# Expert 5's weights issued earlier, gathers issued in a row, and every expert's second layer on TensorE column tiles of 32

## The chip, the core and the metric

The kernel runs on one core of one Trainium2 chip. The core has TensorE (PE, with its weight loads, PEld), VectorE (DVE), ScalarE (ACT), GpSimd (POOL) and SyncE (SP), which only issues transfers here, and 16 DMA engines that move data between HBM and SBUF. The metric is the device time of one execution in microseconds (us), less is better.

## The reference

Attention with normalised queries and keys, and behind it a layer of experts of which each token uses one, and each expert at most 80 tokens:

```python
q_n, k_n = rmsnorm(q, g_q), rmsnorm(k, g_k)          # (8, 12, 448, 64)
attn = softmax(q_n @ k_n.T / sqrt(64))
x = (attn @ v).transpose(0, 2, 1, 3).reshape(3584, 768)
logits = x @ w_gate                                  # 8 experts
expert_idx, gate_w = argmax(logits), softmax(logits) at expert_idx
out = zeros
for e in range(8):
    tok = the 80 tokens of expert e with the largest gate_w
    h = relu(x[tok] @ w1[e])                         # 768 -> 1024
    out[tok] = gate_w[tok] * (h @ w2[e])             # 1024 -> 768
```

## The kernel before

**Attention.** The 8 batches of 12 heads are 24 groups of four heads, worked through in slots of a schedule that is written out by hand. A group's scores (L436), exponentials (L439), sums (L471) and attention products (L453) run over seven blocks of keys. The rows of x go to a scratch tensor in HBM, `xr_scratch`, with the softmax sums' inverses `rz` beside them. The gate and the choice of the 80 tokens per expert are carried from batch to batch (`merge`), and the last batch's choice stands between the attention and the experts (L934 to L1179).

**Weights.** All expert weights are cast to bf16. Experts 0 to 2 are loaded into place during the attention. Experts 3 to 7 are staged in HBM (`wb_scratch`) and fetched by SP: 3 and most of 4 into space that the queries and keys leave (`weights_early`), the rest of 4 and all of 5 into the space that the attention's own tiles leave (`weights_late`, called in the last slot), 6 and 7 into the space of experts 0 and 1, once those are done. An expert's first layer is `w1` (6 x 128 rows of 1024), its second `w2` (8 x 128 rows of 768), 1536 KB each. SP issues in program order, and one issue that waits holds up all behind it. The stack `av_stack` holds, in this order, `vp0` (values, two buffers), `qkT0`, `vp1` (one buffer of values, used by every third group, the last one too), `qkT1`, `attn` (six buffers of exponentials) and `sm`. Into the same space `weights_late` puts the rest of expert 4, then expert 5's `w1` and `w2`; a tile waits for the last reader of what it lies over.

**The last part of expert 5's `w2`.** `fetch_part` fetches six of the eight blocks after the attention's schedule, and the other two when a DVE memset has released them, which stands behind the first multiply of `normal(1)` (L941, L1260).

**Experts.** For expert e, 48 matmuls make the first layer (`ph`, L1249, 80 columns each), ACT applies the relu, and `xpose(e + 1)` turns the next expert's rows (six transposes). `gather(e)` fetches 80 rows of x from `xr_scratch` with an indirect transfer on POOL's queue, and `normal(e)` scales them on DVE. Gathers 2 and 3 are issued after half of expert 0's first layer, 4 to 7 by experts 0 to 3 as their buffers come free. The second layer (L1224) is, for experts 1 to 7, `main`, the first 64 tokens on two column tiles of 64 (16 matmuls of 384 columns), and `rest`, the other 16 tokens on four column tiles of 32, once for two experts (32 matmuls of 384 columns; expert 7's alone has 32 of 192). Expert 0's second layer takes all 80 tokens at once, 16 matmuls of 384 columns, with `xpose(1)` inside it. DVE multiplies by the gate weight (`yo`, `yr`), and POOL scatters the rows into the output (L1217). For the two column tiles the gate weights and row numbers are spread over the partitions by 12 matmuls (`psp`, L1160).

Of the kernel before, what the change touches and what calls it, by code (L numbers as in the profile page):

```python
# [10 lines left out]
F32 = mybir.dt.float32  # L11
BF16 = mybir.dt.bfloat16
AF = mybir.ActivationFunctionType
ALU = mybir.AluOpType
# [7 lines left out]
def kernel(  # L22
# [185 lines left out]
    NE = DC - 1  # L208

# [11 lines left out]
    def chunk(e, i, c):  # L221
        ts = w_tiles[e][i]
        return ts[0][:, c] if len(ts) == 1 or c < NE else ts[1][:, c - NE]

# [48 lines left out]
    vpools, qktpools = [], []  # L273
    for last in range(2):
        vpools.append(av_stack.enter_context(tc.tile_pool(name=f"vp{last}", bufs=2 - last)))
        qktpools.append(av_stack.enter_context(tc.tile_pool(name=f"qkT{last}", bufs=1)))
    apool = av_stack.enter_context(tc.tile_pool(name="attn", bufs=6))
    smpool = av_stack.enter_context(tc.tile_pool(name="sm", bufs=4))
    with av_stack:
# [506 lines left out]
        def weights_late():  # L786
# [3 lines left out]
            load_weights(wlate, NW0 + 2, NW0 + 2)  # L790
            fetch_late(NW0 + 1)
            fetch_late(NW0 + 2, (0, ))
            mlate.append(ctx.enter_context(tc.tile_pool(name="moe_sb", bufs=2)))
# [142 lines left out]
    FE = FC - 2  # L936

    def fetch_part(c, held=False):
        t = w_tiles[NW0 + 2][1][0]
        if held:  # L940
            nc.vector.memset(t[:, c.start, 0:2], 0.0)  # L941
        nc.sync.dma_start(out=t[:, c], in_=staged(NW0 + 2, 1)[:, c])

    fetch_part(slice(0, FE))
# [4 lines left out]
    xbn = [mpool.tile([128, NT, 256], BF16, tag="yo", name="xbn", bufs=3) for _ in range(NQ)]  # L949
# [169 lines left out]
    outs = dram_disjoint_views(out, E + E // 2)  # L1119
# [20 lines left out]
    idxT = tpool.tile([CAP, 1], U32, name="idxT")  # L1140
    nc.vector.tensor_copy(idxT[:, :], psc[:CAP, 1, :1])
# [5 lines left out]
    gwT = rows[:, 0]  # L1147
# [6 lines left out]
    spread = mpool.tile([128, 2 * E + E], F32, tag="spread", name="spread", bufs=1)  # L1154
    psp = [hot[-1][:, 1, :2 * E], hot[-1][:, 1, 2 * E:3 * E]]
    for o, c in enumerate((slice(0, MT), slice(LT, CAP))):
        n = c.stop - c.start
        for p in range(0, 128, n):
            es = slice(1 + p // 64, None, 2) if o else slice(0, E)
            nc.tensor.matmul(psp[o][p:p + n].rearrange("p (c e) -> p c e", c=2), ident[:CAP, c],  # L1160
                             rows[:, :, es], start=(o == 0), stop=(o == 1))
# [9 lines left out]
    nc.vector.tensor_copy(spread[:, :], hot[-1][:, 1, :3 * E])  # L1171
# [4 lines left out]
    idxP = mpool.tile([128, E // 2], U32, tag="idxP", name="idxP", bufs=1)  # L1176
    for c, x, k in ((slice(0, E // 2 - 1), 2.0, 1), (slice(E // 2 - 1, E // 2), 4.0, 2)):
        nc.vector.tensor_scalar(idxP[:, c], spread[:, 2 * E + E // 2:][:, c], x, off[:, k:k + 1],
# [48 lines left out]
    def main(e, py, fcs):  # L1227
        for fc in fcs:
            for n in range(2):
                product(py[MT * n:MT * n + MT, :], e, fc, slice(0, MT),  # L1230
# [113 lines left out]
```

## Time and profile before

| | us |
|---|---|
| median of three runs | 409.56 (407.32 to 410.78) |
| the profiled execution | 410.17 |
| its span, first to last instruction | 408.5 |
| PE busy | 394.2 (96%) |
| DVE busy | 350.1 (86%) |
| ACT busy | 321.0 (79%) |
| POOL busy | 90.7 (22%) |

Times in the rows below are us from the start of the span. "L1249" is a line of the kernel. In a timeline a row merges like instructions that follow each other on one engine; a bracket at its end is the idle time before it and what ended that. PE is busy nearly throughout, so the shares of the whole span tell little; what matters is who waits in the last 60 us. The ends of matmuls are modelled, and a few records are missing.

### The profile page before, as it was taken

The page shows a single profiled execution, that of the slowest core. Times are in us where ns is not written, and L with a number is a line of the kernel's source. Part 1 is how long each engine was busy: PE and PEld are TensorE (multiplying, and loading weights), DVE is VectorE, ACT ScalarE, POOL GpSimd, SP SyncE. Part 2 cuts the span into 40 slices and gives each one's busy share as a digit, 9 for nine tenths or more (in the row PEclk, how much of TensorE's full clock was granted, in tenths as well). Part 3 has the DMA queues.
Part 4 walks back from the last instruction along what each step waited for, and adds up shares of the span by engine and source line. Part 5 has one row for each costly group of instructions (what it writes and reads, how often), then busy time and mean ns, then how long its engine had stood idle before and what let it go on. Part 6 is the DMA issues. An engine that isn't in the chain of part 4 may idle for free.

```text
span 408.5 us, 12889 instructions
## 1 busy us (share of the span) xinstructions
PE 394.2 (96%) x5407; PEld 191.7 (47%) x5407; DVE 350.1 (86%) x654; ACT 321.0 (79%) x510; POOL 90.7 (22%) x161
## 2 busy tenths in 40 slices
PE   8999999999999999999999999999999999999992
PEld 7434444444444444444444444444444453467771
DVE  4899987998999999997999999979999958875641
ACT  5898979997989889988899699979897877572120
POOL 7300002501031012220251024010510020145522
PEclk9999999999999999999999999999999999999999
DMA  7359999999989999989999999999999269788991
GB/s 245 132 168 198 279 291 253 285 212 308 254 221 265 248 256 273 294 183 238 253 302 214 256 252 229 302 233 290 231 275 292 71 216 373 255 235 239 341 359 66
DMA packets 76266, 100.94 MB, mean 247 GB/s; under 512 B 8536, under 2 KB 65376, under 8 KB 76208
## 3 DMA queue, kind: packets, MB, share of 16 engines
q1 hardware_dynamic: 60192, 70.99, 54.5%
q0 software_dynamic: 16016, 29.13, 38.8%
q8 instruction: 42, 0.69, 0.6%
q14 instruction: 16, 0.13, 0.1%
HBM read 101.11 MB, written 40.23 MB: 346 GB/s over the span
## 4 chain that ended last, share of the span: by engine, by line
PE 69%; DVE 12%; ACT 7%; issue 6%; POOL 3%; DMA 1%; POOLq 0%; DVEq 0%
PE ps L436 26%; PE po L453 25%; PE zl L488 5%; DVE sm L471 4%; PE tp L394 4%; PE xp L394 3%; POOL out_dram L1217 2%; DVE ms L327 2%; DVE qn L357 2%; PE wps L908 2%; DMA xg<-xr_scratch,idxG 1%; ACT at L439 1%; ACT qkT L425 1%; PE mp L679 1%; PE mp L394 1%
## 5 line engine op out<-in xcount | busy, mean ns | idle before, releaser
L439 ACT ACTIVATE at<-ps 128x896 f32<-128x896 f32 x168 | 146.6, 931 | 4.5 <-PE ps L436 3.3
L436 PE MATMUL ps<-qkT 64*64 64x448 f32 x1344 | 147.3, 548 | 2.5 <-ACT row L637 1.3
L453 PE MATMUL po<-at,vt 64*64 64x448 f32 x1344 | 142.5, 537 | 0.0
L471 DVE TENSOR_TENSOR sm<-sm,at 128x896 f32<-128x896 f32 x120 | 130.6, 1088 | 3.1
L453 PEld LDWEIGHTS po<-at,vt 64*64 64x64 f32 x1344 | 50.1, 133 | 74.0 <-issue 63.9
L436 PEld LDWEIGHTS ps<-qkT 64*64 64x64 f32 x1344 | 43.8, 132 | 66.6 <-issue 26.2
L327 DVE TENSOR_REDUCE ms<-sq 128x14 f32<-128x896 f32 (+1 forms) x50 | 52.0, 1041 | 6.8 <-ACT sq L320 6.7
L357 DVE TENSOR_TENSOR qn<-qk,rs 128x896 f32<-128x896 f32 (+1 forms) x47 | 50.6, 1078 | 1.3
L320 ACT ACTIVATE sq<-qk 128x896 f32<-128x896 f32 (+1 forms) x48 | 44.7, 931 | 1.9 <-DMA qk<-in_q_dram 1.1
L240 POOL COPY mark<-mark 1x1 bf16<-1x1 bf16 x18 | 7.1, 393 | 132.0 <-DVE mark L239 132.0
L756 ACT COPY xb<-xp 128x1024 f32<-128x1024 f32 x24 | 24.3, 1012 | 8.5 <-PE xp L394 8.4
L394 PEld LDWEIGHTS tp<-ident,qn 64*128 64x128 f32 x672 | 23.5, 139 | 12.1 <-issue 5.3
L394 PE MATMUL tp<-ident,qn 64*128 64x64 f32 x672 | 27.2, 226 | 0.3 <-DVE qn L357 0.3
L460 ACT COPY us<-po 128x896 f32<-128x896 f32 (+1 forms) x24 | 21.4, 893 | 6.5 <-PE po L453 6.5
L469 DVE TENSOR_TENSOR sm<-at 128x896 f32<-128x896 f32 x24 | 26.0, 1083 | 0.1
L1256 ACT ACTIVATE h_sb<-ph 128x320 bf16<-128x320 f32 x16 | 7.0, 437 | 24.2 <-PE ph L1249 22.3
L425 ACT COPY qkT<-tp 128x896 f32<-128x896 f32 x24 | 22.0, 916 | 3.8 <-PE tp L394 3.7
L423 ACT ACTIVATE qkT<-tp,gqk 128x896 f32<-128x896 f32 x23 | 23.5, 1023 | 0.0
L1224 PE MATMUL py<-w_sb,h_sb 128*64 128x384 bf16 (+3 forms) x256 | 18.6, 318 | 2.2 <-DMA w_sb<-wb_scratch 2.2
L488 PE MATMUL zl<-us,wgs 64*32 64x448 f32 x192 | 20.3, 541 | 0.0
L488 PE MATMUL zl<-sm,zsel 64*32 64x448 f32 x192 | 20.1, 540 | 0.0
L394 PEld LDWEIGHTS xp<-ident,us 64*128 64x128 f32 x384 | 14.0, 139 | 12.0 <-ACT at L439 10.6
(214 smaller groups left out, 425.4 us busy)
## 6 DMA issues: line engine op xcount, KB each, us to landing
vt<-in_v_dram SPq DMA_DIRECT2D x24, 448.0 KB, 6.4
out_dram<-zeros SPq DMA_DIRECT2D x28, 384.0 KB, 8.4
w_sb<-wb_scratch SPq DMA_DIRECT2D x7, 1536.0 KB, 14.7
qk<-in_q_dram SPq DMA_DIRECT2D x23, 448.0 KB, 7.0
qk<-in_k_dram SPq DMA_DIRECT2D x23, 448.0 KB, 6.0
w_sb<-in_moe_w_dram POOLq DMA_DIRECT2D x6, 1536.0 KB, 15.7
xr_scratch<-xb SPq DMA_DIRECT2D x48, 192.0 KB, 6.5
wb_scratch<-in_moe_w_dram POOLq DMA_DIRECT2D x12, 768.0 KB, 9.8
```

The lines of the kernel that those rows point to most:

```text
L320: nc.scalar.activation(o, x, AF.Square)
L327: nc.vector.reduce_sum(out=st[g]["ms"][:, a, lo:hi], in_=st[g]["sq%d" % a][:, lo:hi], axis=AX.X)
L357: e.tensor_mul(qn[:].rearrange("p (x hh) d -> p hh x d", hh=2)[:, h0:h1], qk[:, lo:hi].rearrange("p (hh x) d -> p hh x d", x=NX), rs[:, lo ...
L394: nc.tensor.transpose(o, w, one[p, p], tile_position=(p.start, 0))
L425: nc.scalar.copy(T[:], tp[:, :, :S])
L436: nc.tensor.matmul(ps[u * 64:u * 64 + 64, hh, :S], T1[d, u, x * 64:(x + 1) * 64], T0[d, u, :], start=True, stop=True)
L439: nc.scalar.activation(at[:], ps[:, :, :S], AF.Exp)
L453: nc.tensor.matmul(po[u][hh * D:(hh + 1) * D, u, :S], vt[p, hh * NX + x, :], at[p, hh, :], start=(x == 0), stop=(x == RD - 1))
L469: nc.vector.tensor_add(s["sm"][:], s["at0"][:], s["at1"][:])
L471: nc.vector.tensor_add(s["sm"][:], s["sm"][:], s["at%d" % x][:])
L488: nc.tensor.matmul(t[32 * c:32 * c + 32, r, :S], w, x, start=(i == 0), stop=(i == NQ - 1))
L756: nc.scalar.copy(xb[:].rearrange("p j (u hh d) -> p hh (j u) d", u=2, hh=2), xp[:].rearrange("p hh (k d) -> p hh k d", d=D))
```

## The change

It does five things.

1. `vp1` is the last pool of `av_stack` instead of the third, so that expert 5's `w1` lies over `qkT1` and two buffers of `attn`. Expert 5's `w2` is two tiles, of six and of two blocks. The six are fetched in `weights_late`, right behind `w1` and so ahead of the last two groups' stores in SP's queue; the two where the six were fetched before, with no hold.
2. Gathers 3, 4, 5 and 7 are issued right behind gather 2; gather 6 follows in expert 1.
3. `main` runs on four column tiles of 32 (32 matmuls of 384 columns) for every expert.
4. Expert 0 does as the others: `main(0)`, then `xpose(1)`, `yo` and its scatter, then `rest` of expert 0 alone (32 matmuls of 192 columns), `yr` and its scatter, then `normal(2)`. The copy `idxT` is gone, four small matmuls spread expert 0's last 16 tokens, and there is one more index column.
5. The ring of `yo` has four buffers instead of three, and the output one more disjoint view.

```diff
-    for last in range(2):
-        vpools.append(av_stack.enter_context(tc.tile_pool(name=f"vp{last}", bufs=2 - last)))
+    vpools.append(av_stack.enter_context(tc.tile_pool(name="vp0", bufs=2)))
+    for last in range(2):
         qktpools.append(av_stack.enter_context(tc.tile_pool(name=f"qkT{last}", bufs=1)))
     apool = av_stack.enter_context(tc.tile_pool(name="attn", bufs=6))
     smpool = av_stack.enter_context(tc.tile_pool(name="sm", bufs=4))
+    vpools.append(av_stack.enter_context(tc.tile_pool(name="vp1", bufs=1)))
...
             load_weights(wlate, NW0 + 1, NW0 + 1, gst[0]["w"])
-            load_weights(wlate, NW0 + 2, NW0 + 2)
+            w_tiles[NW0 + 2] = ([wlate.tile([128, DC, F], BF16, tag="w1_5", name="w1_sb")],
+                                [wlate.tile([128, n, DM], BF16, tag=f"w2_5{n}", name="w2_sb")
+                                 for n in (FE, FC - FE)])
             fetch_late(NW0 + 1)
             fetch_late(NW0 + 2, (0, ))
+            nc.sync.dma_start(out=w_tiles[NW0 + 2][1][0][:], in_=staged(NW0 + 2, 1)[:, :FE])
...
-    fetch_part(slice(0, FE))
+    nc.sync.dma_start(out=w_tiles[NW0 + 2][1][1][:], in_=staged(NW0 + 2, 1)[:, FE:])
...
-    idxT = tpool.tile([CAP, 1], U32, name="idxT")
-    nc.vector.tensor_copy(idxT[:, :], psc[:CAP, 1, :1])
...
+    for p in range(0, 128, 32):
+        nc.tensor.matmul(hot[-1][p:p + 32, 1, 3 * E:3 * E + 2], ident[:CAP, LT:CAP],
+                         rows[:, :, 0], start=False, stop=True)
...
     def main(e, py, fcs):
         for fc in fcs:
-            for n in range(2):
-                product(py[MT * n:MT * n + MT, :], e, fc, slice(0, MT),
-                        slice(n * DN, n * DN + DN))
+            for n in range(4):
+                t, c = n % 2 * 32, n // 2 * DN
+                product(py[32 * n:32 * n + 32, :], e, fc, slice(t, t + 32), slice(c, c + DN))
...
                 gather(2, ph[:CAP, 0, 0:1])
-                gather(3)
+                for n in (3, 4, 5, 7):
+                    gather(n)
...
-                xn = normal(1, lambda: fetch_part(slice(FE, FC), True))
+                xn = normal(1)
         if 0 < e < E - 1:
             xpose(e + 1, xn)
-        if e < E - 4:
-            gather(e + 4, wait=True)
+        if e == 1:
+            gather(6, wait=True)
...
+        py = sums("py")
+        main(e, py, fcs)
         if e == 0:
...
+            xpose(1, xn)
+        yo = mpool.tile([128, DN], F32, tag="yo", name="yo", bufs=4)
+        nc.vector.tensor_scalar(yo[:, :], py[:, :], gws[:, e:e + 1], None, op0=ALU.mult)
+        scatter(e, idxM[:, e:e + 1], yo[:, :], 2)
+        if e % 2 == 0 or e == E - 1:
+            k = (e - 1) // 2 if e else E // 2
+            g = gwP[:, k:k + 1] if e else spread[:, 3 * E:3 * E + 1]
+            single = e in (0, E - 1)
+            pair = (e, ) if single else (e - 1, e)
             w = len(pair) * DM // 4
             pz = sums("pz")
             rest(pair, pz, fcs)
...
+        if e == 0:
+            xn = normal(2)
```

## Rows read from the trace of the kernel before

**Rows 1.** Timeline of PE, 364 to 403 us: start, us, engine, line, operation, tiles, count
```profile
364.79 0.47 PE L1160 MATMUL hot<-rows,ident 80*64 80x16 f32 x12
365.19 1.89 PE L1249 MATMUL ph<-xgT,w_sb 128*128 128x80 bf16 x48
366.94 2.14 PE L1224 MATMUL py<-w_sb,h_sb 128*80 128x384 bf16 x12
369.32 0.92 PE L1203 MATMUL pxt<-identb,xn 80*128 80x80 bf16 x6 [0.24 <-DVE w_sb L941]
...
370.74 1.88 PE L1249 MATMUL ph<-xgT,w_sb 128*128 128x80 bf16 x48
...
374.19 1.89 PE L1249 MATMUL ph<-xgT,w_sb 128*128 128x80 bf16 x48
...
376.23 2.90 PE L1224 MATMUL py<-w_sb,h_sb 128*64 128x384 bf16 x48
379.07 1.89 PE L1249 MATMUL ph<-xgT,w_sb 128*128 128x80 bf16 x48
...
389.38 0.50 PE L1249 MATMUL ph<-xgT,w_sb 128*128 128x80 bf16 x9 [0.40 <-issue]
...
400.15 1.17 PE L1224 MATMUL py<-w_sb,h_sb 128*64 128x384 bf16 x12 [1.76 <-DMA w_sb<-wb_scratch]
401.79 1.29 PE L1224 MATMUL py<-w_sb,h_sb 128*64 128x384 bf16 x36 [0.47 <-DMA w_sb<-wb_scratch]
```

**Rows 2.** Stretches: busy time (count) of PE, PEld, DVE, ACT, POOL; clock, DMA share, GB/s
```profile
349.60:352.00 2.40, 2.40 (x42) 1.00 (x36) 1.76 (x4) 1.54 (x2) 0.00 (x0) 1.00 0.32 58
...
357.00:362.00 5.00, 4.68 (x52) 2.41 (x48) 4.59 (x17) 4.97 (x20) 2.90 (x6) 1.00 1.04 259
...
366.00:369.30 3.30, 3.09 (x43) 2.26 (x39) 0.63 (x5) 0.87 (x2) 1.81 (x2) 1.00 0.35 92
```

**Rows 3.** Timeline of SP's queue from 348 us: first issue, us until the last
```profile
350.31 0.36 SPq L255 DMA_DIRECT2D w_sb<-wb_scratch  x1
...
359.32 10.36 SPq L942 DMA_DIRECT2D w_sb<-wb_scratch  x2
369.79 9.24 SPq L255 DMA_DIRECT2D w_sb<-wb_scratch  x3
```

**Rows 4.** Timeline of PE and of DVE near 343 us: the last scores and sums
```profile
343.01 1.73 PE L436 MATMUL ps<-qkT 64*64 64x448 f32 x16
...
344.55 4.60 DVE L471 TENSOR_TENSOR sm<-sm,at 128x896 f32<-128x896 f32 x4
```

**Rows 5.** Issues at 358.6, 362.9, 366.7, 370.2 us: count, KB, us to landing
```profile
xr_scratch<-rz SPq DMA_DIRECT2D x1, 3.0 KB, 3.3
...
xg<-xr_scratch,idxG POOLq DMA_INDIRECT x1, 5.9
...
xg<-xr_scratch,idxG POOLq DMA_INDIRECT x1, 3.5
...
xg<-xr_scratch,idxG POOLq DMA_INDIRECT x1, 8.3
```

**Rows 6.** Stretches of the expert loop, columns as in rows 2
```profile
376.42:382.97 6.55, 6.55 (x131) 4.68 (x127) 2.99 (x10) 1.01 (x3) 3.00 (x4) 1.00 1.04 309
382.97:389.38 6.41, 6.01 (x134) 4.56 (x131) 3.69 (x10) 1.31 (x3) 3.07 (x3) 1.00 1.05 331
389.38:395.90 6.52, 6.52 (x127) 4.86 (x131) 3.62 (x8) 1.31 (x3) 1.99 (x2) 1.00 1.05 376
```

**Rows 7.** The page: busy time of the engines; an instruction queue: packets, MB, share
```profile
PE 394.2 (96%) x5407; PEld 191.7 (47%) x5407; DVE 350.1 (86%) x654; ACT 321.0 (79%) x510; POOL 90.7 (22%) x161
...
q8 instruction: 42, 0.69, 0.6%
```

**Rows 8.** DMA queues in 386.8 to 386.9 and 393.1 to 393.2: packets, MB, share
```profile
q8 instruction: 1, 0.02, 68.4%
...
q8 instruction: 1, 0.02, 69.1%
```

## What is predicted, and from what

> **What bounds the kernel now.** I read the tail first, since every edit lies in or just ahead of the expert loop. In PE's timeline [rows 1] the reader is to see that from 365.2 us on PE goes from expert to expert with hardly a gap, and that the last expert then waits: its second layer starts at 400.15 after 1.76 us without work, and stops again for 0.47 us until 401.79, both times for its weights. So the end is set by the transfer of expert 7's second layer, and what follows it (1.29 us of PE, then the scatters) is fixed. Without the two waits, and with one unexplained gap of 0.40 us at 389.38 left in, PE would end some 2.2 us sooner.
>
> Then the stretches of the DMA engines [rows 2]. They are full (share 1.04) in 357 to 362, but at 0.32 in 349.6 to 352.0 and 0.35 in 366.0 to 369.3: 1.6 and 2.1 us of their time are unused. The SP queue shows why [rows 3]. Expert 5's first layer is issued at 350.31; its memory lies over the value tile of the last group, which the last attention product reads. Six eighths of expert 5's second layer follow at 359.32, and the other two wait there for the first multiply of `normal(1)` and go at 369.3; behind them stand experts 6 and 7, from 369.79. The hold lets expert 1's gather through. All later weights then queue one after another until 401.79, so an idle stretch before 369.8 is what could be brought forward.
>
> **Part by part.** *Expert 5's weights.* With `vp1` last in its stack, expert 5's first layer lies over `qkT1` and two `attn` buffers, and the six eighths (now a tile of its own) over three. Their last readers are the scores of 343.01 + 1.73 = 344.7 and the second of four sums that begin at 344.55 and take 4.60 together, so 346.9 [rows 4]. They go out 5.6 and 12.4 us sooner, ahead of the last two groups' stores in the SP queue instead of behind. That fills 349.6 to 352. The last two eighths are issued unheld where the six were, at about 359.3. What is queued behind them: the stores of x and of `rz`, for which expert 1's gather waits. The last of these was issued at 358.6 and took 3.3 us [rows 5], so it landed at 361.9, against the gather's issue at 362.9: 1.0 us of cover. Six eighths are 1.18 MB, 3.1 us at the 376 GB/s of a full stretch [rows 6], against 1.6 us of idle time filled; so the stores land 0 to 3.1 us later. I take 1.7, between the ends, of which 1.0 is covered: the gather starts 0.7 us late.
>
> *Expert 1's gather* took 5.9 us with the weights in flight, expert 2's, in the quiet stretch, 3.5 [rows 5]. Now nothing but the last two eighths (0.39 MB, 1.1 us) lies before it: 3.5 to 5.9, and I take 4.2, since most of its time is quiet. It lands at 362.9 + 0.7 + 4.2 = 367.8 instead of 368.8.
>
> *Gathers 2, 3, 4, 5, 7 in a row.* They cost POOL issue time alone (it was busy 3.0 of 6.5 us [rows 6]); gather 4 took 8.3 us under load [rows 5], and each is needed more than that after its issue except gather 3, needed some 7 us later. At nothing; if gather 3 is late, `normal(3)` is, and with it `yo` of expert 1 on DVE, at most 1 to 2 us of PE.
>
> *Expert 0.* Four spread matmuls more, at 0.47/12 us [rows 1], start it 0.15 us later, at 365.35; the first layer (1.89 us) runs to 367.2. Its second layer was 16 matmuls of 384 columns with 80 rows, 2.14 us for the first 12. Now `main` is 32 of 32 rows and `rest` half a pair's. A pair's 16 + 32 matmuls took 376.23 to 379.07, 2.84 us: 1.42 for each part, so `main` with tiles of 32 is taken at 1.42 for every expert, no gain, and `rest` of one expert at 0.7 (half the columns). `main(0)` ends at 368.6. The turning of expert 1's rows (`xpose`) ended at 369.32 + 0.92 = 370.2, 1.4 after the gather's landing at 368.8, so now at 369.2, and until then PE stands still for some 0.3; `rest(0)` covers the copies, and expert 1 starts at 370.0 instead of 370.74. One scatter more costs POOL and DMA only, and the ring of result tiles, four instead of three, holds both of expert 0's. The idx copy removed was on DVE, covered.
>
> *Weights of 6 and 7.* Expert 6's first layer has only expert 0's first layer ahead of it now: issued at 367.2 instead of 369.79. That is 2.6 sooner, less what now falls into the same stretch and did not: gather 3 and a packet of code more, about 1; and the last two eighths, 1.1, should they still be under way. I take 1.7, bounds 0.5 and 2.7. By the weights alone the end moves by -1.7.
>
> *PE's instructions.* `main` doubles its matmuls: an odd expert goes from 70 matmuls to 86, an even one from 102 to 118; with their weight loads a pair of experts from 344 instructions to 408, in the same 3.45 + 4.88 = 8.33 us (370.74 to 374.19 to 379.07). The page has 5,407 matmuls and as many weight loads, and 42 packets on an instruction queue with 0.69 MB [rows 7]: one packet of 16 KB for every 257 of PE's instructions, so I read them as PE's code arriving in blocks of 256. The gap at 389.38 stands in the middle of 48 like matmuls, after the 39th, with no wait that the profile shows. One packet begins at 386.8, none between 389.38 and 393.1, the next at 393.1 [rows 8]. If the gap is a late block, a block can be used 2.5 us after its packet starts, and a fetch that starts when the block before comes into use takes 3.7 + 2.5 = 6.2 us here. The stretches agree [rows 6]: some 256 instructions took 6.55, 6.41 (with the gap) and 6.52 us. Before, a block lasted 344 in 8.33, so 6.2 us: at the edge. After, 408 in 8.33: 5.2 us. Each block fetched under full DMA then comes about 1.0 to 1.1 us late. No row shows PE asking for code at this rate; the bounds are 0 (no late block) and 2.7 (a fetch of 7.9 us, from the gap's own block if it was asked for 1.5 us before 382.97). I take 1.1, by the row nearest to it.
>
> **The sum.** PE without any wait: expert 1 at 370.0, then three times 3.45 + 4.88 = 25.0, then expert 7 with 1.89 + 1.42 + 0.7, and 0.2 for the end of the last matmul: 399.2, against 401.79 + 1.29 = 403.08 before. Experts 1 to 7 have 3 x 408 + 224 = 1,448 instructions, 5.7 blocks, of which four are asked for and used wholly under load: 4 x 1.1 = 4.4, so 403.6. By the weights: 403.1 - 1.7 = 401.4. The later of the two ends it: +0.5. On the profiled execution (408.5 us of span and 1.7 around it, 410.17) that is 410.7; its median over three runs is 409.56, so **410.1 us**.
>
> **The rivals.** *A, the code keeps up.* Then the weights bind and the end is 1.7 sooner (0.5 to 2.7): 407.9 us. For it: one gap in the whole tail, and the next block in [rows 6] was in time. Against: before, a block had 6.2 us and now has 5.2. The Trainium skill (Runtime: NRT & Kernel Launch, section Instruction fetch mechanics) says that a sequencer fetches its next block of 256 instructions while it executes the current one and that the crossing is mostly hidden; by that rule this rival is the outcome, 407.9. It also gives PE room for 2,048 instructions, and the gap at 389.38, if it is a late block, speaks against so much room.
>
> *B, slower: the code falls further behind.* PE is the only bound, and every block comes as late as the gap's own may have: 7.4 us for a fetch (between 6.2 and 7.9) makes 4 x 2.2 = 8.8, PE ends at 408.0, 4.9 us later than before: 414.5. It decides from a fetch of 7.2 us on. For it: the gathers now stand in a row in front of the same engines. Against: two of three blocks came in 6.5 us or less.
>
> *C, the stores hold up gather 1.* If they land the whole 3.1 us later, it starts 2.1 us late, at 365.0, and under load takes 5.9: 370.9, so expert 1 starts at 373.1 instead of 370.0. PE, behind in code too, ends up to 3.1 later than forecast, but has a block less to wait for (1.1): 0.5 + 3.1 - 1.1 = +2.5, 412.1.
>
> **How the numbers follow.** The forecast 0.5 (its own range 409.0 to 411.2, one late block more or less), A 0.27, B 0.13, C 0.10. Run to run, about 1%, 4.1 us, is what can be told from no change. PE without any wait would be 3.9 sooner, so faster by over 1% needs weights and code both at their best: 0.04. Slower by over 1% is most of B and a little of C: 0.12. Within 1%: 0.84. The range 407.0 to 413.2 takes in A down to its bound of 2.7 and C, and leaves most of B out.
>
> **What would show it.** In the profile of the changed kernel: expert 5's first layer issued near 345 and the share of 349.6 to 352 near 1; gather 1 landing near 367.8, and if past 370, C; expert 6's weights issued near 367.2; `main` and `rest` of a pair still in 2.84 us, if less, the columns were sized wrong; 43 packets on the instruction queue; PE gaps without a wait, some 1 us each and about 256 instructions apart, between 375 and 400. With no such gaps and expert 7 still waiting for its weights it is A. If expert 7's second layer starts without a wait for weights, PE was the later one, as forecast. What would make it wrong altogether: a wait in 345 to 363 from the new memory order that I don't see.

## The result, and the profile after

| | before | after |
|---|---|---|
| median, us | 409.88 (407.32 to 410.78) | 413.99 (413.34 to 414.44) |
| ratio to before | | 1.0109, 95% interval 1.0061 to 1.0158 |
| the profiled execution, us | 410.17 | 414.44 |
| its span, us | 408.5 | 412.7 |
| end of PE's last matmul, us | 403.08 | 407.40 |
| packets on the instruction queue | 42 | 44 |

The forecast was 410.1 us, and its range ended at 413.2. The changed kernel is 4.1 us slower; on two more chips its ratio was 1.0119 (1.0073 to 1.0164) and 1.0160 (1.0106 to 1.0214).

PE's timeline of the changed kernel (start, us, engine, line, operation, tiles, count, and in brackets the idle time before it and what ended that), to lay beside [rows 1]:

```profile
364.75 0.59 PE L1092 MATMUL xT<-stayD,xno 80*128 80x80 bf16 x6 [0.58 <-ACT xno L1031]
...
365.95 1.89 PE L1248 MATMUL ph<-xgT,w_sb 128*128 128x80 bf16 x48
367.77 1.48 PE L1224 MATMUL py<-w_sb,h_sb 128*32 128x384 bf16 x32
370.66 0.92 PE L1203 MATMUL pxt<-identb,xn 80*128 80x80 bf16 x6 [1.40 <-DVE xn L1188]
371.50 0.84 PE L1224 MATMUL py<-w_sb,h_sb 128*32 128x192 bf16 x32
372.28 3.38 PE L1248 MATMUL ph<-xgT,w_sb 128*128 128x80 bf16 x48
377.00 0.91 PE L1203 MATMUL pxt<-identb,xn 80*128 80x80 bf16 x6 [1.34 <-DVE xn L1188]
377.85 1.48 PE L1224 MATMUL py<-w_sb,h_sb 128*32 128x384 bf16 x32
379.26 1.89 PE L1248 MATMUL ph<-xgT,w_sb 128*128 128x80 bf16 x48
...
384.43 0.35 PE L1224 MATMUL py<-w_sb,h_sb 128*32 128x384 bf16 x4 [0.51 <-issue]
...
390.72 0.56 PE L1248 MATMUL ph<-xgT,w_sb 128*128 128x80 bf16 x11 [1.05 <-issue]
...
396.92 0.20 PE L1248 MATMUL ph<-xgT,w_sb 128*128 128x80 bf16 x1 [0.92 <-issue]
...
405.26 2.14 PE L1224 MATMUL py<-w_sb,h_sb 128*32 128x384 bf16 x64
```

Against [rows 1] the time goes like this. Expert 0 starts at 365.95 instead of 365.19: +0.76, of which 0.58 is the wait for the carried tokens' rows (`xno`). From there to expert 1 it takes 6.33 us instead of 5.55: +0.78, with the wait of 1.40 for expert 1's rows. Expert 1, to the start of expert 2, takes 6.98 instead of 3.45: +3.53, of which 1.5 is a first layer of 3.38 instead of 1.89, and 1.34 the wait for expert 2's rows. From expert 2 to the end it takes 28.14 instead of 28.89: -0.75. In that last part the three gaps without a wait cost 2.48 where before there was one of 0.40, and the two waits for expert 7's weights, 2.23 together, are gone. Sum: +4.32.

The stretches (busy time and count of PE, PEld, DVE, ACT, POOL; granted clock, DMA share, GB/s), beside [rows 2]:

```profile
349.60:352.00 2.40, 2.40 (x47) 1.24 (x44) 1.93 (x4) 1.55 (x2) 0.00 (x0) 1.00 0.40 34
...
372.40:374.00 1.60, 1.60 (x27) 1.60 (x27) 0.44 (x2) 0.00 (x0) 1.13 (x2) 0.50 1.04 330
374.00:375.70 1.70, 1.66 (x25) 1.48 (x23) 0.00 (x0) 0.44 (x1) 1.39 (x2) 0.51 1.08 279
```

The idle stretch from 349.6 was to be filled, and its share is 0.40 against 0.32 before. Expert 1's first layer ran at half the clock (0.50 and 0.51, so 1.2 GHz of 2.4). SP's queue shows why nothing was filled, beside [rows 3]:

```profile
350.06 0.36 SPq L257 DMA_DIRECT2D w_sb<-wb_scratch  x1
350.54 0.77 SPq L798 DMA_DIRECT2D w_sb<-wb_scratch  x1
351.70 1.51 SPq L771 DMA_DIRECT2D xr_scratch<-xb  x2
353.27 0.92 SPq L772 DMA_DIRECT2D xr_scratch<-xb  x1
354.28 1.23 SPq L771 DMA_DIRECT2D xr_scratch<-xb  x2
355.56 0.68 SPq L772 DMA_DIRECT2D xr_scratch<-xb  x1
357.06 3.79 SPq L550 DMA_DIRECT2D xr_scratch<-rz  x2
360.92 0.61 SPq L552 DMA_DIRECT2D xr_scratch<-rz  x1
...
367.88 4.88 SPq L257 DMA_DIRECT2D w_sb<-wb_scratch  x2
```

Expert 5's first layer goes out at 350.06, where it was 350.31, and the six eighths half a microsecond behind it, both ahead of the stores. They do not only stand ahead of them in the queue. The waits of SP's queue in 345 to 372 us (line, what it waited for, us in total, times, longest) have a row that before has not:

```profile
SPq L550 <- DMA w_sb<-wb_scratch: 3.4, 2, 2.6
```

The two waits fit one rule, that an issue waits until the transfer eight issues ahead of it in SP's queue has landed. Counted in the rows above, the first `rz` store has expert 5's first layer eight ahead of it (landed 6.9 us after its issue, at 357.0; the store goes out at 357.06), the second has the six eighths (landed after 9.7 us, at 360.2, and the store goes out then). That the program hands out eight semaphores in turn would explain it; it is read from these rows and not tested by itself. Landings of the last `rz` store (issued at 360.92) and of gather 1 (at 366.47), as count, KB and us to landing, beside [rows 5]:

```profile
xr_scratch<-rz SPq DMA_DIRECT2D x1, 3.0 KB, 4.4
...
xg<-xr_scratch,idxG POOLq DMA_INDIRECT x1, 3.6
```

So the last store lands at 365.3 instead of 361.9, and gather 1 is issued 1.15 us behind it, at 366.47 instead of 362.9. The row numbers that the gather also needs (`idxG`) are ready at 362.4, so it is not these that it waits for.

### The profile page after: what moved, and what is told of

Same layout as the page of the kernel before. It is cut to its first block, busy times and chain, and to the rows that moved or that the text cites. A ratio compares the mean times of both kernels' runs of the same rounds, so it can differ in the third digit from the quotient of the medians.

```text
span 412.7 us, 13213 instructions
## 1 busy us (share of the span) xinstructions
PE 395.5 (96%) x5575; PEld 192.5 (47%) x5575; DVE 350.4 (85%) x650; ACT 321.2 (78%) x510; POOL 90.4 (22%) x162
## 4 chain that ended last, share of the span: by engine, by line
PE 68%; DVE 12%; ACT 7%; issue 7%; DMA 4%; POOL 3%; POOLq 0%; DVEq 0%
PE ps L439 26%; PE po L456 25%; PE zl L491 5%; PE tp L397 3%; DVE sm L474 3%; PE xp L397 3%; DVE ms L330 2%; POOL out_dram L1217 2%; DMA xg<-xr_scratch,idxG 2%; DVE qn L360 2%; DMA xo<-xr_scratch,idxO 2%; PE wps L914 2%; ACT at L442 1%; ACT qkT L428 1%; PE mp L682 1%
## 5 line engine op out<-in xcount | busy, mean ns | idle before, releaser
L1248 PE MATMUL ph<-xgT,w_sb 128*128 128x80 bf16 x384 | 17.0, 210 | 2.0 <-issue 2.0
```

## The experiments

Theories: **S**, the weights' part makes stores, `rz` and gather 1 late, and PE's waits for these cost it the clock as well; **H**, the old hold protected gather 2 too, and expert 6's first layer now goes out right behind it; **K**, PE's code, in blocks of 256 instructions, can't keep up with main on four tiles of 32; **R**, a rival, the gathers in a row delay each other. Kernels between two empty rows of the table ran on the same chip, with the kernel before. Ratios are of mean times, the column of times has medians.

| run | what differs from the changed kernel | us | before | ratio (95% interval) |
|---|---|---|---|---|
| u1_weights_back | weights' part undone | 410.96 | 408.18 | 1.0070 (1.0049 to 1.0092) |
| u2_main64 | main on two tiles of 64 | 411.22 | 408.18 | 1.0070 (1.0039 to 1.0101) |
| u3_gathers_back | gathers undone | 414.32 | 408.18 | 1.0143 (1.0077 to 1.0209) |
| s1_ring | ring of exponentials turned | 412.20 | 408.18 | 1.0096 (1.0063 to 1.0128) |
| | | | | |
| r0_changed_again | nothing | 413.23 | 408.39 | 1.0119 (1.0073 to 1.0164) |
| h1_hold | expert 6's first layer held | 413.01 | 408.39 | 1.0109 (1.0060 to 1.0158) |
| u12_weights_main64 | u1 and u2 | 407.66 | 408.39 | 0.9982 (0.9959 to 1.0006) |
| c1_ring_hold_main64 | s1, h1 and u2 | 408.00 | 408.39 | 0.9994 (0.9973 to 1.0016) |
| | | | | |
| n1_halves64 | u1, main as 32 halves on tiles of 64 | 417.80 | 410.17 | 1.0191 (1.0145 to 1.0238) |
| k1_clock | idle matmuls in PE's waits | 418.20 | 410.17 | 1.0201 (1.0157 to 1.0244) |
| a2_before_main32 | (the kernel before, with main on 32) | 413.29 | 410.17 | 1.0083 (1.0050 to 1.0116) |
| c3_ring_hold_main64_early2 | c1, gather 2 not delayed | 419.44 | 410.17 | 1.0234 (1.0196 to 1.0272) |
| | | | | |
| r1_changed_again | nothing | 414.06 | 408.06 | 1.0160 (1.0106 to 1.0214) |
| k2_clock_again | as k1 | 412.25 | 408.06 | 1.0115 (1.0061 to 1.0169) |
| n2_halves64_again | as n1 | 411.28 | 408.06 | 1.0079 (1.0045 to 1.0113) |
| u4_weights_back_again | as u1 | 411.87 | 408.06 | 1.0111 (1.0055 to 1.0167) |
| | | | | |
| u5_weights_main64_again | as u12 | 417.13 | 409.89 | 1.0164 (1.0147 to 1.0181) |
| c4_early2_again | as c3 | 418.88 | 409.89 | 1.0208 (1.0192 to 1.0225) |

### Each part undone

u1 takes back the pools' order, the tiles, the order of the fetches and the hold; u2 takes back

```diff
-            for n in range(4):
-                t, c = n % 2 * 32, n // 2 * DN
-                product(py[32 * n:32 * n + 32, :], e, fc, slice(t, t + 32), slice(c, c + DN))
+            for n in range(2):
+                product(py[MT * n:MT * n + MT, :], e, fc, slice(0, MT),
+                        slice(n * DN, n * DN + DN))
```

and u3

```diff
-                for n in (3, 4, 5, 7):
-                    gather(n)
+                gather(3)
...
-        if e == 1:
-            gather(6, wait=True)
+        if e < E - 4:
+            gather(e + 4, wait=True)
```

> The changed kernel with its first part undone: pools, tiles, the order of the fetches and the hold of expert 5's second layer as before; gathers in a row and column tiles of 32 stay. Theory S (the six eighths ahead of the stores in SP's queue hold up the stores and rz, with them the row gather of the carried tokens and gather 1, and PE's wait for these costs it the clock): the last rz store lands near 361.9 us again instead of 365.35, gather 1 is issued near 362.9 instead of 366.47, expert 1's first layer starts near 370.2 at a granted clock of 1.00 and takes 1.9 instead of 3.38; about 3 us less, some 411 us, with the weights of expert 7 landing near 400 to 402 again and so perhaps ending it. Theory K (PE's code in late blocks is the loss): nothing changes, 414. Theory R (the gathers in a row hold up gather 2): 413 to 414, gather 2 still lands over 8 us after its issue.

> The changed kernel with its third part undone: the second layer's first 64 tokens on two column tiles of 64 (16 matmuls) instead of four of 32 (32 matmuls), expert 0's too. Theory K: the three gaps on PE without a wait (0.51, 1.05 and 0.92 us, 255 or 256 instructions apart) shrink to one or two of 0.4 or less, 42 packets on the instruction queue; 2.0 us less less the slightly longer main (0.1 for a pair): 412. Theory S alone: 413.7 to 414. Both say that expert 1 still starts at 372.3 at half the clock.

> The changed kernel with its second part undone: gather 3 behind gather 2, gathers 4 to 7 issued by experts 0 to 3 as before; weights early and tiles of 32 stay. Theory R (the row of gathers delays gather 2, and through it the turning of expert 2's rows, 1.34 us of wait on PE): gather 2 lands 1 to 2 us sooner, that wait goes, 412.5. Theories S and K: gather 2 is behind expert 6's first layer, not behind the other gathers; 414 within 0.5.

> The changed kernel with the weights' part undone and the second layer's first 64 tokens on two column tiles of 64: of the change only the gathers in a row and expert 0's second layer in two parts are left. Theory K: against the kernel with only the weights' part undone (four gaps on PE without a wait, 1.08, 1.33, 0.92 and 0.20 us, 3.5 together) at most one gap of 0.5 is left, and PE ends near 400, or the weights end it near 400 to 401: 2 to 3 us less than that kernel, within 0.5 us of the kernel before. If the tiles of 32 cost nothing and the gaps come from the gathers in a row: as with only the weights' part undone, 2.8 us above the kernel before.

> The changed kernel as it is, as the base for its variants on one chip. Nothing is told apart by it alone: 1.0 to 1.1% above the kernel before; expert 1's first layer at 372 to 373, at half the clock in some executions, three or four gaps on PE without a wait from 384 on.

Measured: each of u1 and u2 stands 0.70% above the kernel before, u12 with both 0.18% below (the interval holds no change), the changed kernel 1.19%. R falls on this chip: with the gathers taken back it is no faster (1.0143), and gather 2 still takes 9.8 us, with expert 6's first layer issued beside it. K's part can be read in u1's PE timeline, where the rows of experts 1 and 2 are in time:

```profile
369.81 1.89 PE L1250 MATMUL ph<-xgT,w_sb 128*128 128x80 bf16 x48
...
379.18 0.35 PE L1226 MATMUL py<-w_sb,h_sb 128*32 128x384 bf16 x4 [1.08 <-issue]
...
385.74 0.55 PE L1250 MATMUL ph<-xgT,w_sb 128*128 128x80 bf16 x11 [1.33 <-issue]
...
391.94 0.20 PE L1250 MATMUL ph<-xgT,w_sb 128*128 128x80 bf16 x1 [0.92 <-issue]
...
397.58 1.46 PE L1226 MATMUL py<-w_sb,h_sb 128*32 128x384 bf16 x29 [0.20 <-issue]
```

The gaps, 3.53 us together, stand 255 or 256 instructions apart (matmuls and weight loads), and u12, with two tiles of 64, has none and is 0.88% (3.6 us) lower. The timeline of u2 has no gap of that kind either and shows S by itself, here with the first layers of expert 1 in u2 (first) and u12, and u12's two waits for rows:

```profile
372.48 1.90 PE L1248 MATMUL ph<-xgT,w_sb 128*128 128x80 bf16 x48
```

```profile
368.77 1.89 PE L1250 MATMUL ph<-xgT,w_sb 128*128 128x80 bf16 x48
371.45 0.92 PE L1205 MATMUL pxt<-identb,xn 80*128 80x80 bf16 x6 [0.79 <-DVE xn L1190]
...
376.26 0.92 PE L1205 MATMUL pxt<-identb,xn 80*128 80x80 bf16 x6 [0.65 <-DVE xn L1190]
```

Expert 1 starts 3.7 us later with the weights' part, and the times differ by 0.88%, 3.6 us. In the traces less of it reaches the end: PE ends at 402.74 in u2, 402.94 in u1 and 400.72 in u12, so 2.0 and 2.2 us apart, since u12 waits 1.44 us for the rows of experts 2 and 3 (u2's traced run, 409.73, is the lowest of its seven; their median is 411.22). Both theories had u2's expert 1 at half the clock; it ran at 1.00.

So each loss alone is worth 3.6 us by the ratios, and both together the 5.6 that r0 and u12, on one chip, lie apart. That this is less than 7.2 does not show that they overlap: u1 and u2 ran on another chip than u12, the difference is smaller than the intervals of the four ratios together, and by PE's ends the sum comes out the other way (2.0 and 2.2 against the 5.6 between r0's 406.31 and u12's 400.72). (Beside r1 the weights' part undone, u4, gains 2.2 us, as 1.0119 to 1.0070 is 2.0.)

### The ring turned, and the hold given back

s1 puts the last two exponentials into the ring's upper buffers, where expert 5's first layer and the six eighths don't lie; h1 holds expert 6's first layer behind the first multiply of `normal(1)`; c1 has both and two tiles of 64.

```diff
+        for _ in range(3):
+            skip = apool.tile([128, 2, S], F32, tag="at", name="skip")
+            nc.gpsimd.memset(skip[:, 0, 0:2], 0.0)
...
-                xn = normal(1)
+                def held():
+                    w1 = wpool.tile([128, DC, F], BF16, tag="w1_0", name="w1_sb")
+                    w_tiles[E - 2] = ([w1], [])
+                    nc.vector.memset(w1[:, 0, 0:2], 0.0)
+                    fetch_late(E - 2, (0, ))
+                xn = normal(1, held)
...
```

> The changed kernel with the ring of exponential tiles turned by three places (three tiny extra tiles at the start), so that the last two exponentials lie in its two upper buffers and no longer under expert 5's first layer and the six eighths: these no longer wait for the last attention product at 350.0. If the prediction's first step failed only because of that overlap: both are issued near 347 instead of 350.06 and 350.54, fill 349.6 to 352, land near 354.5 and 358, rz 2 is released at 358 instead of 360.28, gather 1 is issued near 363 instead of 366.47, expert 1 starts near 370 at full clock: 410.5 to 411.5. Theory K: 414, whatever lands when. A rival within S: the two transfers now compete with the end of expert 4's (landing 350.9), nothing is gained: 413 to 414.

> The changed kernel with one wait more: expert 6's first layer is held in SP's queue behind the first multiply of normal(1), as expert 5's last two eighths were before; everything else stays. Theory H (what the old hold protected was gather 2 as well; without it expert 6's first layer goes out 0.2 us after gather 2 and gather 2 takes 9 us instead of 3.5): gather 2 lands 3.5 to 4.5 us after its issue, near 372, the turning of expert 2's rows waits for nothing (1.34 us less), the weights of 6 and 7 start 2.5 to 3 us later but were over 5 us early; 1.3 to 2.8 us less than the changed kernel. Theory K (code alone): no difference, within 0.5 us. Theory S (stores late, first gather late, clock): expert 1 starts at 372.3 as before the hold; within 0.7 us of the changed kernel.

> The changed kernel with the ring of exponential tiles turned by three places (the weights really go out near 347), expert 6's first layer held behind the first multiply of normal(1), and two column tiles of 64. If S, H and K together are the whole loss: expert 1 starts near 369.1 at full clock, gather 2 lands within 4.5 us, no gap on PE over 0.5 us, the weights of expert 7 land near 396 to 399 and PE ends at 398 to 400.5 against 403.08: 2 to 4 us less than the kernel before. If something else of the change costs time (the gathers in a row, expert 0 in two parts), it is no faster than the kernel before, and the gap stands in the first 10 us of the expert loop.

SP's queue and PE's timeline of s1:

```profile
346.39 0.36 SPq L257 DMA_DIRECT2D w_sb<-wb_scratch  x1
346.86 0.48 SPq L801 DMA_DIRECT2D w_sb<-wb_scratch  x1
...
358.84 0.47 SPq L555 DMA_DIRECT2D xr_scratch<-rz  x1
...
366.64 2.88 SPq L257 DMA_DIRECT2D w_sb<-wb_scratch  x2
```

```profile
369.05 1.90 PE L1251 MATMUL ph<-xgT,w_sb 128*128 128x80 bf16 x48
373.00 0.92 PE L1206 MATMUL pxt<-identb,xn 80*128 80x80 bf16 x6 [2.05 <-DVE xn L1191]
373.85 2.49 PE L1227 MATMUL py<-w_sb,h_sb 128*32 128x384 bf16 x32
376.27 2.48 PE L1251 MATMUL ph<-xgT,w_sb 128*128 128x80 bf16 x48
```

The overlap was indeed what kept the weights back: they go out at 346.39 and 346.86, the last `rz` store is issued at 358.84, and expert 1 starts at 369.05. But the time is 412.2, not 410.5 to 411.5: now PE waits 2.05 for expert 2's rows, since expert 6's first layer goes out 0.4 us behind gather 2, and the clock is halved there. H is right about the mechanism, and yet h1 alone gains nothing (413.01 against 413.23). Its PE timeline:

```profile
372.30 3.31 PE L1248 MATMUL ph<-xgT,w_sb 128*128 128x80 bf16 x48
375.45 0.38 PE L1203 MATMUL pxt<-identb,xn 80*128 80x80 bf16 x6
...
383.11 0.35 PE L1224 MATMUL py<-w_sb,h_sb 128*32 128x384 bf16 x4 [1.26 <-issue]
...
389.40 0.55 PE L1248 MATMUL ph<-xgT,w_sb 128*128 128x80 bf16 x11 [1.05 <-issue]
...
395.59 0.20 PE L1248 MATMUL ph<-xgT,w_sb 128*128 128x80 bf16 x1 [0.92 <-issue]
```

The wait for expert 2's rows is gone (1.37 in r0), and the gaps are 3.23 instead of r0's 1.25: what PE wins ahead of 380 it waits out at the next blocks of code, which come into use 6.29 and 6.19 us apart (6.29 and 6.20 in the profile after). c1, without S, H and K, has no gap without a wait behind 370 and is at 0.9994: within its interval the whole loss, and no more. Expected were 2 to 4 us below the kernel before and PE's end at 398 to 400.5; PE ends at 401.59, 1.5 us ahead of the trace before, and the times are level. The kernel before has no trace on this chip, so where its 1.5 us went stays open. Waits of 0.28 and 1.03 us for the rows of experts 2 and 3 are left in c1: gather 3 took 8.5 us there and 8.6 in u12, against 3.8 before. In u3, without the row of gathers, it took 10.4, so weights issued beside it are enough for that.

### Instructions or tile shape; the clock by itself

n1 and n2 give main as many instructions as four tiles of 32, on the old two tiles of 64; k1 and k2 keep PE busy in its two waits (results overwritten).

```diff
-        for fc in fcs:
-            for n in range(4):
-                t, c = n % 2 * 32, n // 2 * DN
-                product(py[32 * n:32 * n + 32, :], e, fc, slice(t, t + 32), slice(c, c + DN))
+        for h in range(0, DN, DN // 2):
+            for fc in fcs:
+                for n in range(2):
+                    product(py[MT * n:MT * n + MT, h:h + DN // 2], e, fc, slice(0, MT),
+                            slice(n * DN + h, n * DN + h + DN // 2))
```

```diff
+    def stir(p, n):
+        for _ in range(n):
+            nc.tensor.matmul(p[:, :], identb[:, :],
+                             tri[:, :].unsqueeze(1).to_broadcast([128, 3, 128]),
+                             start=True, stop=True)
...
+            stir(py, 8)
         if 0 < e < E - 1:
             xpose(e + 1, xn)
...
+            stir(pz, 9)
             xpose(1, xn)
...
```

> The changed kernel with the weights' part undone, and the second layer's first 64 tokens on two column tiles of 64 whose 384 columns are taken in two halves: 32 matmuls of 192 columns, as many instructions as with four tiles of 32, in the old tile shape. It tells the number of instructions from the shape of the tile. Theory K (PE's code comes in blocks of 256 that take over 6 us each while the weights are under way): gaps on PE without a wait of about 1 us each, 255 or 256 instructions apart, as with the tiles of 32 (1.08, 1.33 and 0.92 us), and 2 to 3 us above the same kernel with 16 matmuls: 0.5 to 0.8% above the kernel before. If the tile of 32 itself is what costs: no such gap over 0.5 us, and within 0.5 us of the kernel with two tiles of 64, so 0.2% below the kernel before.

> The changed kernel with 17 idle matmuls of 384 columns added where PE waits: nine ahead of the turning of expert 1's rows, eight ahead of the turning of expert 2's; their results are overwritten. Nothing else moves. The clock's price by itself: the granted clock stays at 1.00 from 369 to 380, expert 1's first layer takes 1.9 instead of 3.38 (or its second 1.5 instead of 2.65). If that price reaches the end: 1.5 us less than the changed kernel. Theory K (from 380 on PE can't go faster than its code comes, 256 instructions in 6.2 us): what is won before 380 is lost again in longer gaps behind it, and the end moves by 0.5 us or less.

> The changed kernel as it is, as the base for the clock's price. If the row of gaps at 370 to 376 us belongs to the edits of n1 and k1: 1.0 to 1.2% above the kernel before, as twice before, no gap on PE without a wait ahead of 380. If it belongs to the chip of the third call (with gathers in a row) and this is that chip: 2% above, with such a row; on another chip none of these four has it.

> The changed kernel with 17 idle matmuls of 384 columns where PE waits ahead of the turnings of experts 1 and 2, as in k1_clock. Clock alone decides: 1.5 us less than the changed kernel beside it. Theory K (from 380 on code sets PE's pace): 0.5 us less or nothing, and the gaps behind 380 add up to 1 us more than in the changed kernel. If the row of gaps comes from this edit: 3 to 4 us more than the changed kernel beside it, with the row at 372 to 376 us again.

> The changed kernel with the weights' part undone and 32 matmuls of 192 columns on two tiles of 64, as in n1_halves64. Theory K (the number of instructions): gaps without a wait 255 or 256 instructions apart, 0.9 to 1.3 us each, and a time within 1 us of the kernel beside it with tiles of 32. If the shape of the tile costs: no gaps over 0.5 us, 2 to 3 us less than that kernel. If the row of gaps comes from this edit: 3 to 4 us more than it.

> The changed kernel with the weights' part undone and tiles of 32, as in u1_weights_back, as the base for the run with halves: 0.5 to 0.9% above the kernel before, gaps of 1.1, 1.3 and 0.9 us, 255 or 256 instructions apart from 379 on; 1.5 to 2% above, with a row of gaps at 369 to 374 us, if that row belongs to the chip.

n1 and k1 could not answer: on their chip a row of gaps stood at 369 to 376 us, told of below. Run again as n2 and k2 on the chip of r1 and u4, neither had it, so it doesn't come from the edits. n2's PE timeline:

```profile
369.35 0.93 PE L1226 MATMUL py<-w_sb,h_sb 128*64 128x192 bf16 x18 [0.90 <-issue]
...
382.01 0.35 PE L1226 MATMUL py<-w_sb,h_sb 128*32 128x384 bf16 x4 [1.68 <-issue]
...
388.31 0.55 PE L1251 MATMUL ph<-xgT,w_sb 128*128 128x80 bf16 x11 [0.98 <-issue]
...
394.50 0.20 PE L1251 MATMUL ph<-xgT,w_sb 128*128 128x80 bf16 x1 [0.73 <-issue]
```

Three of its four gaps stand at the same places in the program as in u1 and u4, its first gap stands two blocks of 256 ahead of its second, and the time, 411.28, is within 0.6 us of u4's 411.87. It is the number of instructions, not the tile of 32. For the clock, a stretch of r1 and then one of k2 (columns as above):

```profile
377.40:379.20 1.80, 1.80 (x27) 0.71 (x20) 0.73 (x4) 0.00 (x0) 1.16 (x1) 0.50 1.02 246
```

```profile
375.80:378.00 2.20, 1.94 (x38) 1.10 (x38) 1.79 (x8) 0.00 (x0) 0.59 (x2) 1.00 1.01 240
```

With the clock kept, the second layer of expert 1 takes 1.48 instead of 2.62 and the first of expert 2 1.90 instead of 2.36: 1.6 us. The gaps behind take back 0.24 (1.45 against 1.21), PE ends 1.13 sooner in the profiled runs, and the medians are 1.8 apart. Both theories were partly right: most of the clock's price reaches the end here.

### One part alone in the kernel before

a2 is the kernel before with `main` on four tiles of 32 for experts 1 to 7 (the diff of u2 the other way round).

> The kernel before with one part of the change alone: main on four column tiles of 32 for experts 1 to 7. Theory K: gaps without a wait of 0.9 to 1.3 us, 255 or 256 instructions apart, from 376 on, three or four of them, so PE ends 2 to 3 us later than 403.08, less what it no longer waits for expert 7's weights (up to 2.2): 0.2 to 0.7% above the kernel before. The prediction's own terms for this part (four blocks late by 1.1 each, against 2.2 us of room): 2.2 us above. If code is not the bound: within 0.2% or, by the columns, 0.1% below.

Measured: 0.83% above the kernel before, 3.1 us between the medians. Late blocks cost 1.11 and 0.95 us at 389.46 and 395.93, more small ones before and behind. The direction is K's; its size is read with care, since this is the chip with the row of gaps, of which a2, without gathers in a row, shows only pieces of 0.2 to 0.4 us.

### Gather 2 sooner, and what stays open

c3 is c1 with gathers 2 and 3 right behind gather 1:

```diff
-                gather(2, ph[:CAP, 0, 0:1])
+                gather(2)
```

> The kernel with the ring turned, expert 6's first layer held and two column tiles of 64, and one thing more: gather 2 is no longer delayed until half of expert 0's first layer, so gathers 2 and 3 are issued right behind gather 1, into the stretch where the DMA engines are nearly idle (362 to 367). If late gathers are what is left there (waits of 0.28 and 1.03 us ahead of the turnings of experts 2 and 3): both go, PE ends near 400.3 instead of 401.59, about 1.2 us less than that kernel, 0.3% below the kernel before. If gathers 1 to 3 slow each other: gather 1 lands 1 us later and expert 1 starts later by as much; no gain.

> The changed kernel with the weights' part undone and two tiles of 64, as in u12_weights_main64, timed longer. If the gathers in a row and expert 0 in two parts are worth what PE's timeline gives (expert 0 to the end 36.29 us against 37.89, of which the start of the loop and the tail of the scatters take some back): 0.2 to 0.4% below the kernel before. If they are worth nothing: within 0.1%. On a chip with the row of gaps: 0.5 to 1% above.

> The kernel with the ring turned, expert 6's first layer held, two tiles of 64 and gathers 2 and 3 issued right behind gather 1, as in c3_ring_hold_main64_early2. If the early gathers take away the waits ahead of the turnings of experts 2 and 3 (0.28 and 1.03 us): 1.2 us below c1_ring_hold_main64, 0.3% below the kernel before. If gathers 1 to 3 slow each other: expert 1 starts 1 us later, no better than 0.1% above. If DVE, which holds expert 0's turned rows (1.56 us of wait on PE at 366.20 in the run before), is what the early gathers delay: expert 0 starts 1 to 1.5 us later, 0.2 to 0.5% above.

Both times it was over 2% above the kernel before, and both times on a chip with the row of gaps, so c3 and c4 say nothing sure about early gathers. They do show expert 0 waiting 1.5 us for its turned rows. u5 is u12 on such a chip, 1.64% above the kernel before where 0.5 to 1% were expected. PE's timeline there:

```profile
370.18 0.29 PE L1226 MATMUL py<-w_sb,h_sb 128*32 128x192 bf16 x4 [0.42 <-issue]
370.94 0.33 PE L1226 MATMUL py<-w_sb,h_sb 128*32 128x192 bf16 x5 [0.47 <-issue]
372.40 0.23 PE L1250 MATMUL ph<-xgT,w_sb 128*128 128x80 bf16 x2 [1.13 <-issue]
...
408.06 2.26 PE L1226 MATMUL py<-w_sb,h_sb 128*64 128x384 bf16 x48 [0.99 <-ACT h_sb L1258]
```

Every 0.7 us or a multiple of it PE gets another few instructions, in the middle of a block, while the gathers are in flight; the same program takes 407.66 us on one chip and 417.13 on another, while the kernel before takes 408.39 and 409.89. All five kernels with gathers in a row on these two chips have it, none of the twelve runs on the three other chips has it, nor the profile after. These five also have expert 0 in two parts, which a2 has not, so which of the two brings it is not told apart. What it is, and whether the kernel before has a small piece of it there, stays open. So no version here beats the kernel before: u12 is level with it on one chip and 1.6% above on another.

## Why the prediction was wrong

Beside the forecast's own times, expert 0 started 0.60 us late (365.95 against 365.35) and took 1.68 more (6.33 against 4.65), expert 1 took 3.53 more (6.98 against 3.45), and the rest took 2.01 less (28.14 against 25.75 and the 4.4 for code). So PE ended 3.8 us after the forecast's 403.6, and all of the loss lies ahead of expert 2, where the sum had one wait of 0.3.

**"They go out 5.6 and 12.4 us sooner": the first step that failed.** The instructions of [rows 4] were read rightly, but not which tiles they read. The ring of exponentials turns, and its last two tiles, read by the last attention product, lie under the new place of expert 5's weights. So the first layer went out 0.25 us sooner (350.06 against 350.31) and the six eighths 8.8 (350.54 against 359.32), and of "that fills 349.6 to 352" next to nothing came (0.40 against 0.32); s1 shows the step as it was meant, at 346.39.

**"1.0 us of cover" did not exist.** What looked like room between the last store's landing and gather 1's issue is the way from one to the other: 361.9 to 362.9 [rows 5], and 1.09 to 1.15 us in the nine traces in which that store holds the gather up (365.3 to 366.47 after the change, 361.7 to 362.89 in s1). The last store was 3.4 us late instead of 1.7, a little beyond the 3.1 of the whole six eighths, because the `rz` stores waited for two landings, and all of that reached the gather. Rival C, which the prediction priced with gather 1 landing at 370.9 and expert 1 starting at 373.1, is nearest to what happened: 370.1 and 372.28. The split was another, though: issued at 366.47 and not 365.0, and under way for 3.6 and not 5.9. It was given 0.10.

**"Gathers in a row: at nothing" held; the removed hold did not.** Gather 2's 3.5 us [rows 5] were those of a quiet stretch that the hold kept quiet. The prediction had expert 6's first layer issued at 367.2, half a microsecond beside gather 2, and did not price what that does to gather 2. Now gather 2 is issued at 367.73 and the weights at 367.88; the first multiply on its rows starts at 376.52, 8.8 us later, and PE waits 1.34. Given back by itself, the hold gained nothing (h1), since PE then waited for its code instead.

**The clock was in no step.** PE's waits were counted at their length; behind them the next layer cost up to 1.5 us more, at 0.50.

**Expert 0 and main were sized well.** `main` with tiles of 32 takes 1.42 (377.85 to 379.26) as predicted, `rest` of one expert 0.78 instead of 0.7, expert 0 to expert 1 in u1 4.93 instead of 4.65.

**The weights' end moved by more than -1.7**: the last part, for which PE waits in [rows 1], lands near 397.6 instead of 401.8, and it no longer mattered, as the forecast had it.

**The code was right in kind and nearly in size.** Predicted were blocks of 256, 6.2 us each under full DMA, about 1.1 us late: measured were 1.05 and 0.92 in the profile after, 1.08, 1.33 and 0.92 in u1, and 5.6 to 6.6 us from block to block in these two. The four late blocks (4.4) were three and a bit: 3.53 where PE was in time, 2.48 where it was late already. The rule of the Trainium skill (Runtime: NRT & Kernel Launch, section Instruction fetch mechanics), that crossing to the next block is mostly hidden, is not what these traces show in this stretch; in u12, with 16 instead of 32 matmuls, it holds.

**Rival C's sum was the right kind, and two losses short.** It added the late gather to the late code and took off 1.1 because a late PE waits less for its code; the gaps show as much (3.53 in u1, 2.48 after). It lacks the wait behind the removed hold and the clock. That the time lies near rival B's 414.5 is chance: no trace shows B's fetch of 7.4 us, and the longest way from block to block is 6.57 us (u4).

**What the code alone costs stays partly open.** In u1, with weights and hold as before, PE ends at 402.94, near the forecast's 403.6 and level with the 403.08 of the trace before; yet on its chip u1 is 2.8 us above the kernel before, not 0.5. The one trace of the kernel before is of an execution of 410.17, 2.0 us above its median there. Whether it waits the whole 2.23 us for expert 7's weights in other executions too, or less, so that the room for late code was smaller than taken, no trace shows.

## What to carry to other kernels

Before a transfer is moved ahead of others in a queue, look up which buffers of a rotating pool lie under its target, and who waits eight issues behind it; and time from a landing to the issue that it releases is a way, not room. A hold protects everything issued while it lasts, so ask of each transfer in that stretch how long it would take without it. More matmuls in the same time need more code: where the DMA engines are full, count instructions for each microsecond, here 256 in some 6.2.

## What the runs showed of the hardware

- PE's gaps without a wait stand 255 or 256 of its instructions apart, which is read as code coming in blocks of 256. Under a DMA share of 0.87 to 1.05 a block came into use 5.9 us (r0, k2) to 6.6 us (u1, u4) after the one before; PE stood still for 0.5 to 1.7 us when it was done sooner. With 16 matmuls of tiles of 64 there was no such gap in u2, u12 and c1, and one of 0.40 in the kernel before.
- The granted clock fell to 0.50 or 0.51, so from 2.4 to 1.2 GHz, after PE had waited 1.40 us (after), 1.20 (u3), 1.25 (h1), 2.05 (s1) and, in r0 and r1, after the second of two waits of over 1.3 us each, though not after the first (1.74 and 1.57). It was 1.00 after waits of 0.86 (u2) and 1.03 (c1), and with idle matmuls in the waits (k2).
- On two of the chips, PE stood still without a wait after every few instructions for some 6 us while the row of gathers was in flight, and the last expert's second layer waited 1.0 to 1.1 us for ACT; the same program took 9.5 us more on one chip than on another. The cause is open.
